# Two chained attentions and a three-expert maximum layer: the first layer of batches 2 to 7 as a Strassen scheme of 33 matmuls a tile

## The chip, the cores and the metric

The kernel runs on one core of a Trainium2 chip. The metric is the time of one execution on the device, in microseconds (us). The engines are TensorE (PE, with its weight loads PEld), VectorE (DVE), ScalarE (ACT), GpSimd (POOL) and SyncE (SP), which issues all DMAs here.

## The reference

For each of 8 batches and 8 heads (576 tokens, 64 features), 32 packed queries `p` attend over `k` and `v`; then the 576 queries `q` attend over the 32 packed results, which serve as keys and values. The heads are laid side by side (512 features a token) and go through a layer of three experts, of which the elementwise maximum is kept, and an output layer.

```python
def sm_attn(qq, kk, vv):
    s = scale * np.matmul(qq, kk.transpose(0, 1, 3, 2))
    s = s - np.max(s, axis=-1, keepdims=True)
    a = np.exp(s)
    a = a / (np.sum(a, axis=-1, keepdims=True) + 1e-09)
    return np.matmul(a, vv)
p_packed = sm_attn(p, k, v)
out = sm_attn(q, p_packed, p_packed)
...
h = np.maximum(np.maximum(x @ w1, x @ w2), x @ w3)
return (h @ w_out).astype(np.float32)
```

The four weight matrices are 512 x 768 (three) and 768 x 512.

## The kernel before

**Tiling.** Everything is float32 in and out. `b` is the batch, `j` one of 6 tiles of 128 hidden features, `hf` a half of the tokens (288 = `HS`), `r` the parity of the head (4 even heads and 4 odd ones; 4 heads x 32 packed rows fill 128 partitions). The attention weights over the packed rows stand in `et` (`[128, 576]`, one for each parity), and the second product with the packed values is never formed: `project(b, j)` multiplies the packed values into the experts' weights instead (`pw`, 128 rows x 3 experts x 128 features, for each parity), and `layer_in(b, j)` multiplies `et` by that. So a tile of the first layer is, for each expert and each token half, a sum over the two parities.

**Three matmuls a product.** Each operand is split into a rounded part and a remainder of the type fp32r (`hi`, `lo`; the remainder is the operand less its rounded part): `a2h`, `a2l` from `et`, `ph`, `pl` from `pw`. A product of two operands is three matmuls of 128 x 128 x 288: hi hi, lo hi, hi lo. A tile has 3 experts x 2 halves x 2 parities = 12 products, 36 matmuls (line 475), into six PSUM banks, one for each expert and half. `maximum(b, j, hf)` copies expert 0's bank to SBUF (`r`) and joins the other two with a maximum on DVE (line 489): 2 copies and 4 joins a tile.

**The rest of a batch.** `halves` and `operands` form the operands `ya`, `yb`, `yc` of the output layer out of pairs of tiles; `layer_out` is a Strassen scheme already, 126 matmuls (line 544); `finish` joins its products and stores. For the next batch `scores`, `weigh`, `invert`, `spread`, `values`, `packed`, `queries` and `attend` make its attention meanwhile.

**Buffers.** PSUM has 8 banks: `ps_moe` gives single ones (4) to the first layer's sums, the output layer's products and some projections, `ps_big` gives two pairs to the scores, the other projections and the attention. SBUF tiles under one tag share a number of slots; tag `y` has 21.

**Order.** Each step is a generator that issues a few instructions at a time. Two strings of words, `START` and `LOOP`, written out as tables, say which generator goes on next: `N01` is `layer_in(b, 1)`, `E010` `maximum(b, 1, 0)`, `P`, `H`, `O`, `F`, `A`, `B` are `project`, `halves`, `layer_out`, `finish`, `weigh_and_turn` and `attend`; a letter `v`, `g` or `a` behind a word puts its elementwise instruction on DVE, POOL or ACT. Each engine takes its instructions strictly in this order and waits on semaphores. `START` holds batches 0 and 1 and the preparation of batch 2; `LOOP` runs six times, for the first layer and the output layer of batches 2 to 7 with the attention of the batch after.

```python
with tc.manual_schedule():
    run(START, 0)
    for b in range(2, B):
        run(LOOP, b)
```

Of the kernel before, what the change touches and what calls it, by code (L numbers as in the profile page):

```python
# [53 lines left out]
C22 B011v B001 E010 A11 A11 A10 A10 E010 Z11 B001v C21 C20 C21 C22 N00 B001v B011 E000 A10 A11 q10 A10v E000
q11 A11 N00 B011g B011 B011 V101 C20 C30 C30 w31 B011 Z10 E010 N01 V101 C21 C21 K1 C30 N00 w52 C31 K1v C32 C32
Q1 N00 E011 E001 B10 C31 w41 P02 P02 B11 C52 P10 P10 B10 w40 B11 k20 C40 C41 C31 P02 N01 E011 C30 N01 C31 P03
B10 P03 E001 E001 C41 N02 N02 E020 N02 C52 N02 E011 k21 N02 H00 w42 B10 B11 P10 E021 P03 S2 C40 E020 C40 N03
N03 N03 v21 C41 C41 C42 E020 B11 C42 B10 E021 C52 E030 C42 A20 A20 A21 A21 w50 C50 w51 B11 B11 B10 X2 X2 C50
C50 C51 N02 C52 N03 C40 C42 P04 C51 C50 B10 E030 E030 P11 B11 N03 B11g N03 C51 B10g P04 C51 P04 E031 N04 N04
N04 P05 E031 B11 v20 B11 E040v E040 B10 H01 H01v N04 N04 N04 E021 w61 C61 E031 P05 E041 P05 N05 N05 N05 E040  # L60
w60 C60 B10g B10 B11 H00 N10 C61 E041 P11 Z20 E050 H00v X2 C60 C60 E041 C61 E050 P11 V201 Z21 V201 N11 N11 K2
w64 N10 C61 E110v E110 E050 H01 H01 w65 C65 C65 N11 q21 N11 N10 K2 E100v N10 H04v H04 q20 Q2 N11 w62 N10 E111
E110 C60 W0v N10 W0v W0v W0 w63 W0 H02v H02 E101 C65 P13 H04v B20 E100 B21 E101 C65 W0 E111 E100 P12 N11 C62
# [628 lines left out]
```

## Time and profile before

| | |
|---|---|
| median of 3 runs | 467.01 us (466.97 to 467.24) |
| span of the profiled execution, first to last instruction | 464.4 us |
| its own time | not given apart from the span; the runs lie 2.6 us above it |
| instructions | 11561, of them 4724 matmuls |
| PEld, share of the span | 87% |
| HBM read and written | 41.94 MB and 9.44 MB, 111 GB/s over the span |
| share of the chain that ended last | PE 88%, DMA 5%, SP's queue 3%, DVE 3%, ACT 1% |

How to read it: a group's row names the line, the engine, the operation, output and inputs by the program's names, the shapes and the count; then the summed time in us, the mean of one in ns, and the idle time before them with what ended it. Rows of the timeline begin with the start and the length in us. The chain is followed back from the last instruction to what released each. A row by stretch has the stretch, its length, then the busy time and count of PE, PEld, DVE, ACT and POOL, the granted clock, the DMA share and GB/s.

### The profile page before, as it was taken

The page shows a single profiled execution, that of the slowest core. Times are in us where ns is not written, and L with a number is a line of the kernel's source. Part 1 is how long each engine was busy: PE and PEld are TensorE (multiplying, and loading weights), DVE is VectorE, ACT ScalarE, POOL GpSimd, SP SyncE. Part 2 cuts the span into 40 slices and gives each one's busy share as a digit, 9 for nine tenths or more (in the row PEclk, how much of TensorE's full clock was granted, in tenths as well). Part 3 has the DMA queues.
Part 4 walks back from the last instruction along what each step waited for, and adds up shares of the span by engine and source line. Part 5 has one row for each costly group of instructions (what it writes and reads, how often), then busy time and mean ns, then how long its engine had stood idle before and what let it go on. Part 6 is the DMA issues. An engine that isn't in the chain of part 4 may idle for free.

```text
span 464.4 us, 11561 instructions
## 1 busy us (share of the span) xinstructions
PE 455.2 (98%) x4724; PEld 404.9 (87%) x4724; DVE 333.5 (72%) x698; ACT 159.9 (34%) x341; POOL 247.9 (53%) x213
## 2 busy tenths in 40 slices
PE   7999998999999999999999999999999999999996
PEld 3477887899899898998899988998989988998996
DVE  1799987888887678566887479766786668845552
ACT  2787856535322126022331025121260223302130
POOL 0468875574542675526572384706764275725832
PEclk9999999999999999999999999999999999999999
DMA  8999846010316430256004450065202540020002
GB/s 313 398 382 355 321 98 230 1 58 25 95 66 195 135 119 1 80 160 233 2 27 152 87 211 2 27 199 155 94 1 94 151 116 1 28 76 1 2 6 97
DMA packets 35780, 55.66 MB, mean 120 GB/s; under 512 B 17296, under 2 KB 26512, under 8 KB 35728
## 3 DMA queue, kind: packets, MB, share of 16 engines
q1 hardware_dynamic: 35728, 54.93, 35.4%
q8 instruction: 37, 0.61, 0.5%
q14 instruction: 15, 0.12, 0.1%
HBM read 41.94 MB, written 9.44 MB: 111 GB/s over the span
## 4 chain that ended last, share of the span: by engine, by line
PE 88%; DMA 5%; SPq 3%; DVE 3%; issue 1%; ACT 1%; DVEq 0%
PE mi L475 44%; PE mo L544 29%; PE pw L439 6%; PE idle L143 2%; SPq L319 2%; PE s L366 2%; PE av L337 2%; DMA wi<-in_wi 2%; PE s L253 2%; DMA q<-in_qt 1%; DMA kt<-in_kp 1%; PE tp L296 0%; DMA xt<-x 0%; SPq L159 0%; PE pa L337 0%
## 5 line engine op out<-in xcount | busy, mean ns | idle before, releaser
L475 PE MATMUL mi<-a2h,ph 128*128 128x288 f32 x576 | 173.5, 301 | 0.8 <-DVE pl L452 0.6
L475 PE MATMUL mi<-a2l,ph 128*128 128x288 f32 x576 | 169.9, 295 | 0.0
L475 PE MATMUL mi<-a2h,pl 128*128 128x288 f32 x576 | 169.6, 295 | 0.0
L489 DVE TENSOR_TENSOR r<-mi,r 128x288 f32<-128x288 f32 x192 | 84.4, 452 | 57.8 <-PE mi L475 55.3
L475 PEld LDWEIGHTS mi<-a2h,ph 128*128 128x128 f32 x576 | 108.0, 188 | 13.4 <-issue 7.0
L475 PEld LDWEIGHTS mi<-a2l,ph 128*128 128x128 f32 x576 | 108.0, 188 | 0.2
L475 PEld LDWEIGHTS mi<-a2h,pl 128*128 128x128 f32 x576 | 108.1, 188 | 0.0
L513 POOL TENSOR_TENSOR r<-r 128x288 f32<-128x288 f32 (+1 forms) x47 | 50.4, 1083 | 81.3 <-DVE r L489 65.5
L129 ACT COPY r<-mi 128x288 f32<-128x288 f32 x73 | 29.0, 399 | 185.8 <-PE mi L475 185.7
L450 ACT ACTIVATE ph<-pw 128x384 fp32r<-128x384 f32 (+1 forms) x67 | 40.2, 631 | 46.5 <-PE pw L439 43.5
L452 DVE SCALAR_TENSOR_TENSOR pl<-pw,ph 128x384 fp32r<-128x384 f32 (+1 forms) x67 | 46.2, 713 | 9.5 <-ACT ph L450 9.2
L544 PE MATMUL mo<-ych,xl 128*128 128x288 f32 x144 | 42.5, 295 | 0.0
L544 PE MATMUL mo<-ych,xh 128*128 128x288 f32 x144 | 42.4, 294 | 0.0
L544 PE MATMUL mo<-ycl,xh 128*128 128x288 f32 x144 | 42.3, 294 | 0.0
L439 PE MATMUL pw<-w_sb,pt 64*32 64x384 f32 x768 | 36.3, 487 | 0.1
L206 POOL TENSOR_TENSOR w_sb<-w_sb,wi 128x512 int32<-128x512 int32 x18 | 23.9, 1336 | 22.0 <-DVE w_sb L202 17.4
L134 POOL TENSOR_TENSOR ybl<-r,ybh 128x576 fp32r<-128x576 f32 x15 | 21.7, 1448 | 19.7 <-DVE ybh L131 16.2
L134 POOL TENSOR_TENSOR ycl<-r,ych 128x864 fp32r<-128x864 f32 x12 | 26.6, 2218 | 5.1 <-PE mi L475 2.4
L544 PE MATMUL mo<-yah,xh 128*128 128x288 f32 x96 | 28.9, 301 | 0.0
L544 PE MATMUL mo<-yal,xh 128*128 128x288 f32 x96 | 28.4, 296 | 0.2 <-DVE yal L134 0.2
L544 PE MATMUL mo<-ybh,xh 128*128 128x288 f32 x96 | 28.3, 295 | 0.0
L544 PE MATMUL mo<-yah,xl 128*128 128x288 f32 x96 | 28.3, 295 | 0.0
(123 smaller groups left out, 808.4 us busy)
## 6 DMA issues: line engine op xcount, KB each, us to landing
kt<-in_kp SPq DMA_DIRECT2D x16, 640.0 KB, 5.4
q<-in_qt SPq DMA_DIRECT2D x16, 576.0 KB, 5.6
wi<-in_wi SPq DMA_DIRECT2D x18, 512.0 KB, 8.6
v<-in_va SPq DMA_DIRECT2D x16, 512.0 KB, 5.7
wi<-in_wo SPq DMA_DIRECT2D x6, 512.0 KB, 6.7
out_t<-r SPq DMA_DIRECT2D x8, 288.0 KB, 2.2
out_t<-t SPq DMA_DIRECT2D x8, 288.0 KB, 2.3
out_t<-s SPq DMA_DIRECT2D x8, 288.0 KB, 2.7
```

Of the source, the lines that this page charges most:

```text
L129: e.copy(out=out, in_=src)
L134: on(default).tensor_tensor(out=lo, in0=src, in1=hi.bitcast(F32), op=ALU.subtract)
L143: nc.tensor.matmul(out=ps[:, 0:n * P], lhsT=ident, rhs=ident.unsqueeze(1).to_broadcast([P, n, P]), start=True, stop=True,)
L206: nc.gpsimd.tensor_tensor(out=dst.bitcast(I32), in0=dst.bitcast(I32), in1=up, op=ALU.add)
L253: nc.tensor.matmul(out=s1[b][r][32 * n:32 * n + 32, hf, 0:HS], lhsT=kt[g][o, w:w + NP], rhs=kt[g][o, pr * S + hf * HS:pr * S + (hf + 1) * HS],
L439: nc.tensor.matmul(out=ps[r][NP * n:NP * n + NP, 0:NW * P], lhsT=pt_sb[b % 2][o, NP * n:NP * n + NP], rhs=w_sb[o, j, n * NW * P:(n + 1) * ...
L450: nc.scalar.activation(out=hi[:, r], in_=x, func=AF.Copy, scale=2.0 ** -WS)
L452: nc.vector.scalar_tensor_tensor(out=lo[:, r], in0=x, scalar=2.0 ** -WS, in1=hi[:, r].bitcast(F32), op0=ALU.mult, op1=ALU.subtract,)
L475: nc.tensor.matmul(out=sums[b, j, hf, x][:, 0:HS], lhsT=w[:, r, x * P:(x + 1) * P], rhs=a[:, c], start=(r == 0 and n == 0), stop=(r == R - ...
L489: nc.vector.tensor_tensor(out=h, in0=sums[b, j, hf, i][:, 0:HS], in1=h, op=ALU.max)
L513: less = lambda out, x, y: on("g").tensor_tensor(out=out, in0=x, in1=y, op=ALU.subtract)
L544: nc.tensor.matmul(out=ps[:, 0:HS], lhsT=w[:, x, m * P:(m + 1) * P], rhs=h[:, z], start=(p == 0 and i == 0), stop=(p == NQ - 1 and i == 2),)
```

## The change

For batches 2 to 7 (`b >= FAST`), experts 0 and 1, the two parities and the two token halves are taken as a 2 x 2 block product and computed with 7 products in place of 8 (Strassen's scheme in Winograd's form); expert 2 keeps its 4. A tile is then 11 products, 33 matmuls. What goes with it:

- `replace(j)`, once for each tile: in `w_sb`, expert 1's weights of the even heads become expert 0's less expert 1's (64 x 512).
- `project` also makes float32 copies `pf` of experts 0 and 1 on ACT, three combinations of 128 x 128 for each tile, and their split `sh`, `sl`.
- `differences(b)`: four instructions overwrite the halves of `et` by differences, which are split as `th`, `tl`.
- `layer_in_fast` fills five banks a tile: `e` (expert 2, half 0), `x`, `u`, `y`, `f` (expert 2, half 1). Some are read while they are filled: after its first two products `e` is copied to `h[0]`, then ACT writes x's first product into it, and PE adds expert 0's second product to that.
- `maximum_fast` does it in 4 copies and 6 joins a tile. A term that two sums share is added after their maximum.
- `START` and `LOOP` are written anew, with other engines for many elementwise steps.

```diff
+    def replace(j):
+        w = w_sb[0:64, j].rearrange("p (n i x) -> p n i x", n=4, i=NW)
+        on("g").tensor_tensor(out=w[:, :, 1], in0=w[:, :, 0], in1=w[:, :, 1], op=ALU.subtract)
+        yield 0
...
     def project(b, j):
...
+        if b >= FAST:
+            f = pool.tile([P, R, 2 * P], F32, name=f"pf{b}_{j}", tag="y", bufs=NY)
+            for r, x in zip(parts, src):
+                nc.scalar.activation(out=f[:, r], in_=x[:, :, 0:2 * P], func=AF.Copy, scale=2.0 ** -WS)
+                yield 1
...
+        combine(1, 3, 1, ALU.subtract)
+        yield 1
+        combine(0, 0, 1, ALU.add)
+        yield 1
+        combine(2, 2, 1, ALU.subtract)
+        yield 1
+        hi = pool.tile([P, 3, P], F32R, name=f"sh{b}_{j}", tag="y", bufs=NY)
+        copy(hi, f[:, 0:3])
+        yield 1
+        lo = pool.tile([P, 3, P], F32R, name=f"sl{b}_{j}", tag="y", bufs=NY)
+        split_lo(lo, f[:, 0:3], hi)
...
+    def differences(b):
+        e = [loaded["et", b, r] for r in range(R)]
+        c = slice(0, HS), slice(HS, S)
+        def less(r, h, x, y):
+            on("g").tensor_tensor(out=e[r][:, c[h]], in0=e[x[0]][:, c[x[1]]], in1=e[y[0]][:, c[y[1]]], op=ALU.subtract)
+        less(0, 0, (0, 1), (0, 0))
+        less(0, 1, (1, 1), (0, 1))
+        less(1, 1, (1, 1), (0, 0))
+        less(1, 0, (1, 0), (1, 1))
+        for r in range(R):
+            hi = pool.tile([P, S], F32R, name=f"th{b}_{r}", tag="y", bufs=NY)
+            copy(hi, e[r])
+            lo = pool.tile([P, S], F32R, name=f"tl{b}_{r}", tag="y", bufs=NY)
+            split_lo(lo, e[r], hi)
...
+    def layer_in_fast(b, j):
+        def product(ps, w, x, first=False):
+            for n, (wi, xi) in enumerate(((0, 0), (1, 0), (0, 1))):
+                nc.tensor.matmul(
+                    out=ps[:, 0:HS], lhsT=w[wi], rhs=x[xi], start=first and n == 0, stop=n == 2,
...
+        product(e, a(0, 2), v(0, 0), first=True)
+        product(e, a(1, 2), v(1, 0))
+        product(x, a(0, 0), v(0, 0), first=True)
+        product(u, a(0, 1), t(0, 1), first=True)
+        product(bank("y"), s(2), v(1, 1), first=True)
+        product(x, s(1), t(1, 1))
+        product(e, a(1, 0), v(1, 0))
+        product(u, a(1, 1), t(1, 0))
+        product(x, s(0), t(0, 0))
+        product(f, a(0, 2), v(0, 1), first=True)
+        product(f, a(1, 2), v(1, 1))
...
+    def maximum_fast(b, j):
+        copy(h[0], of("e"))
+        copy(of("e"), of("x"))
+        copy(h[1], of("u"))
+        join(h[1], of("y"), h[1])
+        copy(u, of("x"))
+        join(h[0], of("e"), h[0])
+        join(u, of("u"), u, ALU.add)
+        join(h[0], u, h[0])
+        join(h[1], of("x"), h[1], ALU.add)
+        join(h[1], of("f"), h[1])
...
-S1 A10 N00 E000 A11 N01 v10 E010v A10 N00 N00 N00 N00 N00 X1 A11 X1 v11 N02 N02 N02 N02 N02 E000 X1 Z10 E001
+S1 A10 A10 N00 N00 E00a A11 N00 N00 q11 P05 E00a A11 N00 N00 E00v E00 E00a N00 N00 N01 N00 X1 X1 E00 E00 E00g
```

(Between the calls of the new functions stand yields, one a word of the table.)

The order on PE, in the pass of batch 4, tile 4, after the matmuls `s2` of the next batch's queries. Before, six matmuls in a row fill one bank (`mi`, with batch, tile, half, expert):

```order
L366 MATMUL s2_5_1_3957<-q11_3868,pt1_74 32x288 x4
L475 MATMUL mi4_4_1_0_3967<-a2h4_0_3511,ph4_4_3850 128x288
L475 MATMUL mi4_4_1_0_3967<-a2h4_0_3511,pl4_4_3851 128x288
L475 MATMUL mi4_4_1_0_3967<-a2l4_0_3551,ph4_4_3850 128x288
L475 MATMUL mi4_4_1_0_3967<-a2h4_1_3444,ph4_4_3850 128x288
L475 MATMUL mi4_4_1_0_3967<-a2h4_1_3444,pl4_4_3851 128x288
L475 MATMUL mi4_4_1_0_3967<-a2l4_1_3495,ph4_4_3850 128x288
```

After, three at a time go to the banks `mx`, `mu`, `my`, and then to `mx` a second time:

```order
L373 MATMUL s2_5_1_4163<-q11_3801,pt1_74 32x288 x4
L530 MATMUL mx4_4_4172<-a2h4_0_3622,ph4_4_4071 128x288
L530 MATMUL mx4_4_4172<-a2h4_0_3622,pl4_4_4072 128x288
L530 MATMUL mx4_4_4172<-a2l4_0_3665,ph4_4_4071 128x288
L530 MATMUL mu4_4_4188<-th4_0_3708,ph4_4_4071 128x288
L530 MATMUL mu4_4_4188<-th4_0_3708,pl4_4_4072 128x288
L530 MATMUL mu4_4_4188<-tl4_0_3716,ph4_4_4071 128x288
L530 MATMUL my4_4_4197<-a2h4_1_3643,sh4_4_4176 128x288
L530 MATMUL my4_4_4197<-a2h4_1_3643,sl4_4_4194 128x288
L530 MATMUL my4_4_4197<-a2l4_1_3669,sh4_4_4176 128x288
L530 MATMUL mx4_4_4172<-th4_1_3721,sh4_4_4176 128x288
```

The second visit to `mx` now stands behind six matmuls of other banks, and waits for ACT's copy of `mx` into `me`.

The order on DVE, at the same place of the pass. Before:

```order
L452 SCALAR_TENSOR_TENSOR pl4_5_3890<-pw4_5_3763,ph4_5_3889 128x768
L489 TENSOR_TENSOR r4_1_3714<-mi4_3_1_2_3914,r4_1_3714 128x288
L489 TENSOR_TENSOR r4_2_3887<-mi4_4_0_1_3923,r4_2_3887 128x288
L489 TENSOR_TENSOR r4_2_3887<-mi4_4_0_2_3930,r4_2_3887 128x288
L389 STREAM_TRANSPOSE e5_1_4002<-s2_5_0_3948 128x288
L389 STREAM_TRANSPOSE e5_1_4002<-s2_5_1_3957 128x288
L389 STREAM_TRANSPOSE e5_0_4020<-s2_5_0_3948 128x288
L389 STREAM_TRANSPOSE e5_0_4020<-s2_5_1_3957 128x288
L393 TENSOR_REDUCE m2_5_0_0_4023<-e5_0_4020 128x18
L395 TENSOR_TENSOR e5_0_4020<-e5_0_4020,m2_5_0_0_4023 128x576
```

After:

```order
L396 STREAM_TRANSPOSE e5_1_4183<-s2_5_0_4154 128x288
L396 STREAM_TRANSPOSE e5_1_4183<-s2_5_1_4163 128x288
L400 TENSOR_REDUCE m2_5_1_0_4186<-e5_1_4183 128x18
L574 TENSOR_TENSOR r4_2_4180<-my4_4_4197,r4_2_4180 128x288
L574 TENSOR_TENSOR r4_2_4180<-me4_4_4133,r4_2_4180 128x288
L574 TENSOR_TENSOR u4_4_4209<-mu4_4_4188,u4_4_4209 128x288
L396 STREAM_TRANSPOSE e5_0_4231<-s2_5_0_4154 128x288
L396 STREAM_TRANSPOSE e5_0_4231<-s2_5_1_4163 128x288
L574 TENSOR_TENSOR r4_2_4180<-u4_4_4209,r4_2_4180 128x288
L574 TENSOR_TENSOR r4_2_4180<-mx4_4_4172,r4_2_4180 128x288
L574 TENSOR_TENSOR r4_2_4180<-mf4_4_4224,r4_2_4180 128x288
```

The joins of a tile are six, one of them (`r<-u,r`) between two SBUF tiles, and the attention's transposes are parted among them.

The order on POOL from one batch's output layer into the next batch's first layer. Before:

```order
L590 TENSOR_TENSOR u_3_3471<-u_3_3471,t_3_3437 128x576
L592 TENSOR_TENSOR t_3_3437<-v_3_3508,t_3_3437 128x576
L513 TENSOR_TENSOR r4_0_3584<-r4_0_3584 128x288
L131 CAST yah4_0_3745<-r4_0_3584 128x576
L134 TENSOR_TENSOR yal4_0_3754<-r4_0_3584,yah4_0_3745 128x576
```

After:

```order
L736 TENSOR_TENSOR u_3_3624<-u_3_3624,t_3_3564 128x576
L738 TENSOR_TENSOR t_3_3564<-v_3_3705,t_3_3564 128x576
L141 TENSOR_TENSOR tl4_0_3716<-et4_0_3620,th4_0_3708 128x576
L141 TENSOR_TENSOR tl4_1_3723<-et4_1_3638,th4_1_3721 128x576
L473 TENSOR_TENSOR pf4_1_3544<-pf4_1_3544 128x128 x3
L138 CAST sh4_1_3729<-pf4_1_3544 128x384
L473 TENSOR_TENSOR pf4_2_3535<-pf4_2_3535 128x128 x2
L141 TENSOR_TENSOR sl4_1_3733<-pf4_1_3544,sh4_1_3729 128x384
L138 CAST sh4_2_3735<-pf4_2_3535 128x384
L141 TENSOR_TENSOR sl4_2_3737<-pf4_2_3535,sh4_2_3735 128x384
```

Eleven instructions for the new operands stand between the output layer's last sums and the first difference of `r4_0`.

More of the change, by code (lines that the diff above doesn't have):

```diff
@@ L36 @@
 WS = 8
+FAST = 2
 NX, NB, NY = 6, 8, 21
@@ L54 @@
[L54 to L63, printed above, removed]
@@ L85 @@
+P10 P10 P10 B10 H04g O0 O0 P05 P05 B10v B11a H05a H05v H05g H05v P12 P12 H03a F0 P11 P10g H05a B10 F0 P10g
+H03v O0 F0 O0 F0 P10g B11 B10v O0 O0 H05v O0 F0 F0 P10a P10g B10 B10a F0 O0 F0 B11g B11 P11 B11a O0 O0 B10g
+T1v T1v B11v T1v T1g k20 O0 O0 O0 F0 F0 T1a P12 P12g P11 F0 F0 T1g F0 F0 T1a T1g F0 P11g P11g P11g P11g P12g
+P12g P11g P12g P11 P11 P12g P12 P12 P12 P11 O0 F0
 """
@@ L455, in project, with combine @@
             yield 1
-    sums, hidden, hid = {}, {}, {}
+        if b < FAST:
+            return
+        f = f.rearrange("p r (i x) -> p (r i) x", i=2)
+        def combine(k, x, y, op):
+            on("g").tensor_tensor(out=f[:, k], in0=f[:, x], in1=f[:, y], op=op)
+        combine(1, 3, 1, ALU.subtract)
[5 more added lines that the diff above has]
+        hi = pool.tile([P, 3, P], F32R, name=f"sh{b}_{j}", tag="y", bufs=NY)
@@ new lines, in maximum_fast, with join @@
+    def maximum_fast(b, j):
+        if (b, j // 2) not in hidden:
+            hidden[b, j // 2] = pool.tile([P, 4, HS], F32, name=f"r{b}_{j // 2}", tag="b", bufs=NB)
+        h = [hidden[b, j // 2][:, 2 * (j % 2) + hf] for hf in range(2)]
+        of = lambda name: sums[b, j, name][:, 0:HS]
+        def join(out, x, y, op=ALU.max):
+            nc.vector.tensor_tensor(out=out, in0=x, in1=y, op=op)
+        copy(h[0], of("e"))
+        yield 0
+        copy(of("e"), of("x"))
+        yield 0
+        copy(h[1], of("u"))
+        yield 0
+        join(h[1], of("y"), h[1])
+        yield 0
+        u = pool.tile([P, HS], F32, name=f"u{b}_{j}", tag="y", bufs=NY)
+        copy(u, of("x"))
+        yield 0
+        join(h[0], of("e"), h[0])
+        yield 0
+        join(u, of("u"), u, ALU.add)
+        yield 0
+        join(h[0], u, h[0])
+        yield 0
+        join(h[1], of("x"), h[1], ALU.add)
+        yield 0
+        join(h[1], of("f"), h[1])
+        yield 0
@@ L459, in layer_in @@
     def layer_in(b, j):
+        if b >= FAST:
+            yield from layer_in_fast(b, j)
+            return
         p_hi, p_lo = pw[b, j]
@@ L479, in layer_in, with maximum @@
                 yield 0
-    def maximum(b, j, hf):
+    def maximum(b, j, hf=None):
+        if b >= FAST:
+            yield from maximum_fast(b, j)
+            return
         if (b, j // 2) not in hidden:
@@ L613, in fused_kernel @@
         "B": attend, "C": convert, "P": project, "N": layer_in, "E": maximum, "H": halves,
-        "O": layer_out, "F": finish, "W": weights,
+        "T": differences, "R": replace, "O": layer_out, "F": finish, "W": weights,
     }
@@ L631, in run @@
                 continue
-            if kind not in "wCW":
+            if kind not in "wCWR":
                 x[0] += base
```

88 lines of the change are left out of this document (66 added, 22 removed).

## The prediction

> **What bounds the kernel now.** I read the page first, for the balance of the engines, then the chain that ended last.
>
> ```profile
> PE 455.2 (98%) x4724; PEld 404.9 (87%) x4724; DVE 333.5 (72%) x698; ACT 159.9 (34%) x341; POOL 247.9 (53%) x213
> ```
>
> The page alone does not prove that PE is the bound, since its matmuls are pipelined. The chain in order of time does. One pass of the loop over batches, from one batch's scores to the next, reads:
>
> ```profile
> 303.82 1.13 PE s L253 x32
> 304.95 14.51 PE mi L475 x108
> 319.46 2.10 PE pw L439 x48
> 321.56 1.39 PE av L337 x80
> 322.95 2.56 PE mi L475 x18
> 325.51 0.11 PE av L352
> 325.62 4.76 PE mi L475 x36
> 330.39 1.13 PE s L366 x32
> 331.52 7.36 PE mi L475 x54
> 338.88 2.10 PE pw L439 x48
> 340.97 16.87 PE mo L544 x126
> 357.85 1.13 PE s L253 x32
> ```
>
> Every piece is PE and each begins where the last ended: a pass is 54.03 us of matmuls without a hole. The pace is 14.51/108 = 0.134 us a matmul, not the 0.295 us that the groups show as the length of one: that is latency. Next, the busy time by stretch, for a pass and for the end of the opening:
>
> ```profile
> 303.82:357.85 54.03, 54.03 (x592) 49.31 (x598) 38.45 (x81) 14.63 (x34) 28.51 (x24) 1.00 0.33 102
> 100.00:120.00 20.00, 20.00 (x153) 20.00 (x152) 16.02 (x32) 7.49 (x14) 10.41 (x10) 1.00 0.14 49
> 120.00:140.00 20.00, 20.00 (x184) 18.53 (x183) 18.22 (x32) 6.78 (x13) 11.06 (x8) 1.00 0.28 93
> ```
>
> After the length come PE, PE's weight loads, DVE, ACT and POOL. In a pass DVE has 15.6 us left over, POOL 25.5, ACT 39.4. The granted clock is 1.00. What the change takes comes off the bound; what it adds must fit into those remainders.
>
> Prices of single instructions, by form, and two joins back to back:
>
> ```profile
> L489 DVE TENSOR_TENSOR r<-mi,r 128x288 f32<-128x288 f32 x192 | 84.4, 452 | 57.8 <-PE mi L475 55.3
> L129 ACT COPY r<-mi 128x288 f32<-128x288 f32 x73 | 29.0, 399 | 185.8 <-PE mi L475 185.7
> L450 ACT ACTIVATE ph<-pw 128x384 fp32r<-128x384 f32 x38 | 16.7, 495 | 41.0 <-PE pw L439 41.0
> L452 DVE SCALAR_TENSOR_TENSOR pl<-pw,ph 128x384 fp32r<-128x384 f32 x38 | 19.0, 538 | 9.2 <-ACT ph L450 9.2
> L513 DVE TENSOR_TENSOR r<-r 128x288 f32<-128x288 f32 x14 | 7.0, 501 | 0.0
> L134 DVE TENSOR_TENSOR yal<-r,yah 128x576 fp32r<-128x576 f32 x10 | 8.2, 818 | 0.5 <-ACT yah L129 0.5
> L134 DVE TENSOR_TENSOR ycl<-r,ych 128x864 fp32r<-128x864 f32 x12 | 12.6, 1054 | 0.0
> L134 POOL TENSOR_TENSOR yal<-r,yah 128x576 fp32r<-128x576 f32 x14 | 20.3, 1449 | 2.5 <-ACT yah L129 1.6
> L218 POOL TENSOR_TENSOR xt<-xb,xt 128x256 f32<-128x256 f32 x2 | 1.5, 739 | 0.8 <-DVE xl L134 0.8
> L129 ACT CAST yah<-r 128x576 fp32r<-128x576 f32 x11 | 7.4, 674 | 2.8 <-PE mi L475 2.1 <-DVE u L563 0.7
> L266 DVE TENSOR_REDUCE mx<-s 128x1 f32<-128x576 f32 x16 | 12.0, 752 | 11.6 <-PE s L253 11.6
> L271 ACT ACTIVATE a<-s,nm 128x576 f32<-128x576 f32 x16 | 11.8, 744 | 7.2 <-DVE nm L267 7.2
> L313 DVE STREAM_TRANSPOSE x<-a 128x576 f32<-128x576 f32 x12 | 8.9, 771 | 0.0
> 221.31 0.81 DVE L489 TENSOR_TENSOR r<-mi,r 128x288 f32<-128x288 f32 x2
> ```
>
> The pair takes 0.81 us and one 0.45, so in a row a 288-column DVE instruction costs a step of 0.37; I take 0.08 off the others likewise.
>
> **The change, part by part.** *Products.* 36 becomes 33 matmuls a tile, six tiles a batch, six batches: 18 x 0.134 = 2.4 us a pass, 14.5 us in all, on the path directly. An all-hidden remainder would give 467.0 - 14.5 = 452.5.
>
> *DVE, a pass.* Joins go from 24 to 36: 12 x 0.37 = 4.5. Two more copies from PSUM: 0.7. Three half-differences of the attention weights at 0.42: 1.3. Four 128-column combinations at 0.2 (an estimate, the step scaled by columns; ends 0.1 and 0.4): 0.8. One split of a combination 0.5, one more `r<-r` 0.4, one each more of `yal`, `ybl`, `ycl`: 0.7 + 0.7 + 1.0. Two casts leave for ACT: -0.9. Sum 9.7, so 38.45 + 9.7 = 48.1 of a pass of 51.6: 93%.
>
> *POOL, a pass.* 14 combinations at 0.45 (estimate between 0.37, half the 256-column row, and 0.74): 6.3. Five splits at 1.05 (between the 0.74 and 1.45 rows): 5.2. Two `tl` at 1.45, two casts and a difference: 4.9. Five casts, four splits and an `r<-r` leave: -9.8. So 28.5 + 6.6 = 35.1, 68%.
>
> *ACT, a pass.* Ten more PSUM copies at 0.4, nine `pf` at 0.45 (between the 0.40 and 0.50 rows), thirteen casts new or taken over at 0.67: 4.0 + 4.1 + 8.7 = 16.8, so 31 of 51.6. Not a bound.
>
> *The new chain inside a tile.* Before, a product bank was filled once and read once. Now `e` is copied out, gets x's partial sum written into it by ACT, and is added to by PE; `u` and `x` are read between additions. PE is in order, so everything behind such a matmul waits. PE gives room of its own: between x's first product and its second stand `u` and `y`, 6 x 0.134 = 0.8 us, against two ACT copies of 0.4, of which the first starts 0.4 us sooner while x is computed. I laid the four orders of one pass side by side and added the rows' durations down them by hand, with 0.2 us from a last matmul's issue to its reader (0.16 of it is 0.295 less 0.134).
>
> Tile 0 as the example, in us from the end of the scores. PE: `e` to 0.8, `x` 1.2, `u` 1.6, `y` 2.0, projection P5 (2.10/3) 2.7, second `x` 3.1, third part of `e` 3.5, second `u` 3.9, third `x` 4.3, tile 1's `e` 5.1, `f` 5.9, tile 1's `x` 6.3. ACT: exponential 1.0 to 1.8, copy of `e` to 2.1, `e<-x` to 2.5; PE's second `x` comes at 2.7: room 0.2. DVE: two maxima with a small instruction each to 1.9, copy of `u` 2.2, join of `y` 2.6, two transposes 4.0, joins of `e` 4.4, `u` 4.8, `r<-u,r` 5.3, `x` 5.7, which frees a bank that PE wants at 6.3: room 0.6. Behind that `x` stand on DVE the copy of tile 1's `e`, which ACT waits for before it can fill that bank, and the join of `f`.
>
> Room at most such places is 0.1 to 0.6 us. It is negative at four: the two banks behind the projection P3, where ACT issues two `pf` and two `ph` (about 1.5 us) and DVE two `pl` (0.54 each) before PE gets them back: 0.1; the second bank of P4, which waits for DVE's `r<-mx` of tile 2: 0.35; the banks behind P4: 0.3; the first output product, which waits for tile 5's joins behind an `e<-e,m`: 0.15. Sum 0.9 us a pass. Ends: 0 and all 2.4.
>
> *DVE held by POOL.* This trace shows something that speaks against the change:
>
> ```profile
> 62.15 2.85 POOL L134 TENSOR_TENSOR a2l<-et,a2h 128x576 fp32r<-128x576 f32 x2
> 64.16 1.45 DVE L134 TENSOR_TENSOR yal<-r,yah 128x576 fp32r<-128x576 f32 x1
> 103.93 0.75 DVE L395 TENSOR_TENSOR e<-e,m 128x576 f32<-128x576 f32 x1
> 223.94 2.31 POOL L513 TENSOR_TENSOR r<-r 128x288 f32<-128x288 f32 x2
> 225.60 1.26 DVE L395 TENSOR_TENSOR e<-e,m 128x576 f32<-128x576 f32 x1
> 445.59 1.37 DVE L134 TENSOR_TENSOR ybl<-r,ybh 128x576 fp32r<-128x576 f32 x1
> ```
>
> The split at 64.16 ended at 65.61, 0.61 after POOL's ended at 65.00; the subtraction at 225.60 took 1.26 beside POOL and 0.75 at 103.93 without. Of the 26 DVE instructions with two SBUF operands that started while POOL ran, 14 (the first at 64.16, the last at 445.59) were held, all with 0.24 us or more of a POOL tensor-tensor still to go. A pass has 8 such DVE instructions and loses 0.5 us to this; it will have 26, and POOL goes from 28.5 to 35.1: 0.5 x 26/8 x 35.1/28.5 = 2.0 us. With it DVE is at 50.1 of 51.6. A hold-up costs PE only where the room is smaller than it; of the 2.0 I take 0.2, ends 0 and 2.0. The Trainium skill (SBUF — State Buffer, section "SBUF: two separate sides") has the pair of ports that DVE and POOL share as an exclusive lock for the whole instruction; by that rule the trace agrees, each of the 14 waits lasted to POOL's end.
>
> *The opening.* The first two batches keep their 36 products. It gets DVE net 4.9: four differences of attention weights 1.7, four `pf` combinations 0.8, four weight differences at 0.6 (estimate between the 288 and 576-column rows) 2.4; splits and casts that move between DVE, POOL and ACT come out even. The two stretches above have 5.8 us of DVE left, but most additions stand in the second, which has 1.8: some 3 us run over into the first pass, whose DVE has 3.5 left. Ends 0 and 4.9; I take 1.0. Today's loop begins here:
>
> ```profile
> 141.74 1.13 PE s L253 x32
> ```
>
>
> *The last pass* has no attention work beside it, and the way out of its first layer is the old one:
>
> ```profile
> 443.58 0.46 DVE r L489
> 444.04 0.68 DVE yal L134
> 444.76 15.89 PE mo L544 x118
> ```
>
> PE waits 1.2 us there, for a join and a split. The split goes from DVE to POOL, 0.7 longer, but it needs tile 4 alone, and 8 matmuls of the output layer (1.07 us) stand ahead of the one that reads it; I leave the wait as it is and take 0.2 for what remains of the other waits: 2.4 - 0.2 = 2.2 saved. SP's queue gets no DMA; the `xt` transfers follow the same two transposes, one join later in DVE's order.
>
> *Sum.* Five passes of 2.4 - 0.9 - 0.2 = 1.3: 6.6 with the unrounded 2.42. Last pass 2.2, opening -1.0: 7.8 us. The profiled span is 464.4, so 456.6; the median of the runs, 467.01, lies 2.6 above the span, which I carry over: 459.2.
>
> **Rivals.** *Everything hides.* For it: 0.1 to 0.6 us of room at most places, and a wait that shifts PE once also gives the next ones room. Against: 93% of DVE. Below 455, down to 452.5; chance 0.13.
>
> *The bank releases eat the gain.* 36 releases a pass at 0.067 us are 2.4 us. For it: the four negative places; an error of 0.1 us in what I take for a reader's delay would make half the others negative. Against: a late matmul gives the readers time. 465 to 469; chance 0.13.
>
> *DVE becomes the bound through POOL's hold.* If the 26 fall at random on POOL's 68%, each loses half a POOL instruction (35.1/39 = 0.9): 26 x 0.68 x 0.45 = 8.0 us, DVE 56.1, a pass 2.1 longer than today; five of them, 10.4 - 2.2 + 1.0: 476. It decides from 54.0 - 48.1 = 5.9 us of hold a pass. Against: today's 8 lose 0.5 and at random would lose 8 x 0.53 x 0.6 = 2.5. Chance 0.12. By the Trainium skill's rule (same section) nothing softens this: the one that starts first keeps the ports.
>
> **How the numbers follow.** My own case, 455 to 465, gets 0.62. A difference under 0.2% (0.9 us) is about what cannot be told from no change. Faster by more: my case, full hiding, and a little of the bank case: 0.80. Same: 0.06, from the bank case. Slower: POOL's hold and the bank case's end: 0.14. The range leaves out the bottom of full hiding (0.05) and most of the slower cases (0.13): 453.5 to 468.
>
> **What would show it.** A pass of about 52.7 us between two batches' scores; 4616 matmuls; DVE at 47 to 50 us a pass, POOL near 35; PE idle of about 1 us a pass put down to DVE `r<-mx`, `pl` and `r<-my`. Wrong: pieces of DVE longer than 1 us in the chain of a pass, `r<-u,r` well over 0.5 us on average (POOL's hold), or a loop that begins later than 142.7.

## The result and the profile after

The changed kernel takes 471.78 us (median of 4 runs, 470.56 to 473.20) against 466.99 us for the kernel before, run beside it (4 runs, 466.92 to 467.24): 1.0105 times as long, 95% interval 1.0082 to 1.0129. The prediction was 459.2 us, with a range from 453.5 to 468.0. The profiled execution took 473.20 us with a span of 471.4, 7.0 more than before; it is the slowest of the four, and the spans of the others are 468.8 to 470.0.

The engines over the whole span:

```profile
PE 457.4 (97%) x4616; PEld 393.2 (83%) x4616; DVE 392.1 (83%) x856; ACT 250.3 (53%) x536; POOL 279.8 (59%) x292
```

The 108 matmuls that the scheme saves are gone, 4616 in place of 4724. Next come the stretches from one batch's scores to the next, five passes and then the last with the end (stretch, length, then PE, PEld, DVE, ACT, POOL):

```profile
143.32:196.85 53.53, 53.53 (x573) 47.25 (x580) 47.38 (x105) 29.29 (x66) 33.45 (x37) 1.00 0.35 103
196.85:251.04 54.19, 54.03 (x573) 47.28 (x579) 48.06 (x105) 29.08 (x65) 34.43 (x40) 1.00 0.35 102
251.04:306.65 55.61, 54.49 (x574) 47.52 (x581) 48.30 (x105) 29.08 (x65) 34.34 (x40) 1.00 0.36 99
306.65:362.42 55.77, 54.54 (x573) 47.54 (x579) 47.52 (x105) 29.12 (x65) 34.42 (x40) 1.00 0.34 99
362.42:417.00 54.58, 54.07 (x567) 47.45 (x567) 48.27 (x105) 29.02 (x65) 34.34 (x40) 1.00 0.26 77
417.00:471.40 54.40, 47.77 (x373) 43.74 (x371) 33.31 (x71) 19.55 (x45) 28.09 (x31) 1.00 0.11 39
```

A pass was 54.03; now the five are 53.5 to 55.8, and the last pass with the end is 54.4 in place of 52.5. The busy times are what was forecast: DVE 47.4 to 48.3, POOL 33.5 to 34.4, ACT 29. PE's busy time counts its short stalls as busy (53.53 of 53.53), so I cut each pass by the starts of the matmuls: the time from the first of a block to the first of the next, summed by kind, in us.

| | before | pass 1 | 2 | 3 | 4 | 5 |
|---|---|---|---|---|---|---|
| products of the first layer (216, now 198) | 29.29 | 28.03 | 28.44 | 28.42 | 28.50 | 28.50 |
| projections `pw` (96, in 2 groups, now 4) | 4.19 | 4.92 | 4.91 | 4.90 | 4.89 | 4.91 |
| `av` | 1.41 | 1.41 | 1.70 | 3.17 | 3.25 | 2.14 |
| scores, both | 2.26 | 2.26 | 2.26 | 2.26 | 2.26 | 2.26 |
| output layer | 16.87 | 16.90 | 16.89 | 16.85 | 16.88 | 16.75 |

With 18 x 0.134 = 2.41 us less the products would take 26.88. They take 1.2 to 1.6 more, the projections 0.7 more, and `av` up to 1.8 more. The chain that ended last shows that third one, in pass 3 (start, length, what):

```profile
253.17 0.41 PE mx L530 x3
253.58 0.17 SPq L181
...
253.79 0.75 SPq L172
...
255.15 8.63 DMA v<-in_va
263.78 0.02 issue
263.80 0.59 SPq L326
...
270.00 1.92 DMA xt<-x
271.92 0.14 issue
272.06 1.41 PE av L344 x74
```

PE's `av` waits for the last of 16 `xt` transfers. SP issues them one after another at some 0.65 us, and ahead of the seventh it stood still for 2.3 us, until a v load of 8.6 us had landed. SP's waits at these issues, before and after (wait in us, times, longest), and the landing of v (count, KB, median us):

```profile
SPq L319 <- DMA v<-in_va: 0.5, 1, 0.5
v<-in_va SPq DMA_DIRECT2D x16, 512.0 KB, 5.7
```

```profile
SPq L326 <- DMA v<-in_va: 10.1, 9, 2.3
v<-in_va SPq DMA_DIRECT2D x16, 512.0 KB, 7.9
```

### The profile page after: what moved, and what is told of

It is laid out like the page before. It is cut to its first block, busy times and chain, and to the rows that moved or that the text cites. A ratio compares the mean times of both kernels' runs of the same rounds, so it can differ in the third digit from the quotient of the medians.

```text
span 471.4 us, 11957 instructions
## 1 busy us (share of the span) xinstructions
PE 457.4 (97%) x4616; PEld 393.2 (83%) x4616; DVE 392.1 (83%) x856; ACT 250.3 (53%) x536; POOL 279.8 (59%) x292
## 4 chain that ended last, share of the span: by engine, by line
PE 76%; DMA 10%; SPq 5%; DVE 3%; ACT 2%; issue 2%; POOL 1%; POOLq 0%; DVEq 0%; ACTq 0%
PE mo L690 27%; PE mi L617 9%; PE mx L530 7%; PE me L530 6%; PE pw L446 6%; DMA v<-in_va 5%; PE mf L530 4%; PE mu L530 4%; SPq L326 4%; PE my L530 3%; PE idle L150 2%; PE s L373 2%; PE s L260 2%; PE av L344 2%; DMA wi<-in_wi 2%
## 5 line engine op out<-in xcount | busy, mean ns | idle before, releaser
L141 POOL TENSOR_TENSOR sl<-pf,sh 128x384 fp32r<-128x384 f32 x30 | 32.5, 1093 | 42.0 <-ACT sh L136 24.6
L473 POOL TENSOR_TENSOR pf<-pf 128x128 f32<-128x128 f32 x80 | 37.5, 481 | 13.8 <-ACT pf L456 12.5
L617 PE MATMUL mi<-a2h,ph 128*128 128x288 f32 x144 | 44.3, 307 | 1.2 <-DVE r L635 1.2
L617 PE MATMUL mi<-a2h,pl 128*128 128x288 f32 x144 | 42.5, 295 | 0.3 <-DVE pl L464 0.3
L617 PE MATMUL mi<-a2l,ph 128*128 128x288 f32 x144 | 42.5, 295 | 0.0
L617 PEld LDWEIGHTS mi<-a2h,ph 128*128 128x128 f32 x144 | 27.0, 188 | 8.6 <-issue 2.3
L530 PE MATMUL me<-a2h,ph 128*128 128x288 f32 x108 | 32.7, 303 | 0.0
L530 PE MATMUL me<-a2h,pl 128*128 128x288 f32 x108 | 31.9, 295 | 0.0
L530 PE MATMUL me<-a2l,ph 128*128 128x288 f32 x108 | 31.8, 294 | 0.0
L690 PE MATMUL mo<-ybl,xh 128*128 128x288 f32 x96 | 28.3, 295 | 0.0
```

The lines of the kernel that those rows point to most:

```text
L141: on(default).tensor_tensor(out=lo, in0=src, in1=hi.bitcast(F32), op=ALU.subtract)
L473: on("g").tensor_tensor(out=f[:, k], in0=f[:, x], in1=f[:, y], op=op)
L530: nc.tensor.matmul(out=ps[:, 0:HS], lhsT=w[wi], rhs=x[xi], start=first and n == 0, stop=n == 2, skip_group_check=not first,)
L617: nc.tensor.matmul(out=sums[b, j, hf, x][:, 0:HS], lhsT=w[:, r, x * P:(x + 1) * P], rhs=a[:, c], start=(r == 0 and n == 0), stop=(r == R - ...
L690: nc.tensor.matmul(out=ps[:, 0:HS], lhsT=w[:, x, m * P:(m + 1) * P], rhs=h[:, z], start=(p == 0 and i == 0), stop=(p == NQ - 1 and i == 2),)
```

## The experiments

Each kernel ran beside the kernel before on the same chip; the median of that one was 466.5 to 467.1 us each time, and the ratios are taken against it. Kernels are compared by the cut of their passes as well, since the time at which the loop begins varies from profile to profile (see e5). How far one profile's passes can be trusted is seen where two kernels have the same program in passes 1 to 5 and differ in the last alone (e6 and e9, e7 and e8, e12 to e15): passes 1 and 5 agree within 0.1 us, passes 2 to 4 differ by up to 0.9. The passes, in us, and the last pass from its first product to its first output product:

| kernel | time | ratio to before, interval | loop begins | passes 1 to 5 | last |
|---|---|---|---|---|---|
| before | 467.0 | | 141.7 | 54.0 54.0 54.0 54.0 53.9 | 31.7 |
| after | 471.8 | 1.0105 (1.0082 to 1.0129) | 143.3 | 53.5 54.2 55.6 55.8 54.6 | 32.7 |
| e1 | 469.0 | 1.0050 (1.0032 to 1.0068) | 143.5 | 53.5 54.0 54.0 54.4 53.9 | 32.6 |
| e2 | 472.3 | 1.0120 (1.0094 to 1.0146) | 142.7 | 54.1 54.6 54.7 55.7 54.5 | 33.0 |
| e3 | 474.1 | 1.0162 (1.0132 to 1.0192) | 142.7 | 54.7 54.8 54.8 56.2 54.7 | 32.6 |
| e5 | 469.3 | 1.0055 (1.0032 to 1.0077) | 144.2 | 54.1 54.1 54.1 54.1 54.0 | 31.7 |
| e6 | 466.6 | 0.9985 (0.9970 to 0.9999) | 142.4 | 53.2 54.1 53.1 54.0 53.0 | 32.8 |
| e7 | 472.1 | 1.0107 (1.0091 to 1.0122) | 143.6 | 53.9 54.2 53.9 55.1 53.8 | 33.8 |
| e8 | 471.1 | 1.0105 (1.0082 to 1.0127) | 143.9 | 53.9 53.9 53.9 54.6 53.8 | 33.8 |
| e9 | 471.3 | 1.0094 (1.0079 to 1.0109) | 142.6 | 53.2 53.5 53.1 53.2 53.1 | 38.8 |
| e10 | 470.1 | 1.0079 (1.0057 to 1.0102) | 143.5 | 53.1 53.2 53.1 53.3 53.1 | 37.0 |
| e11 | 468.6 | 1.0048 (1.0033 to 1.0062) | 141.3 | 54.4 54.6 54.4 54.4 54.3 | 32.0 |
| e12 | 467.4 | 1.0000 (0.9979 to 1.0021) | 142.9 | 53.2 53.3 53.2 53.7 53.0 | 34.8 |
| e13 | 465.3 | 0.9975 (0.9957 to 0.9992) | 141.8 | 53.1 53.2 53.5 53.8 53.1 | 32.7 |
| e14 | 467.2 | 1.0012 (0.9993 to 1.0031) | 142.2 | 53.1 53.3 53.4 53.2 53.1 | 34.2 |
| e15 | 467.1 | 1.0008 (0.9993 to 1.0022) | 144.6 | 53.1 53.2 53.2 53.6 53.1 | 34.1 |

**e1: the q load behind the `xt` transfers.** The new table has the word `q11` ahead of `v11` and `v10`; the old one had it behind the `xt` issues.

```diff
-        nc.sync.dma_start(out=loaded["q", b, g][:, :, c], in_=...)
+        later.append((out, in_))        # for g == 1 of batches 3 to 7
...
         (end of spread, behind the 16 xt transfers)
+        for out, in_ in later: nc.sync.dma_start(out=out, in_=in_)
```

> The changed kernel with one load moved on SyncE's queue: the q load of 576 KB that the new loop issues ahead of the v loads now stands behind the 16 xt transfers. Theory A (the xt transfers are late because a q load and four v loads share the bandwidth just ahead of them, the v loads then take 8 us, and the fifth to ninth xt issue wait for them): av stops waiting in passes 2 to 6 of the loop, which gives back the 0.2, 1.75, 1.85 and 0.75 us that the 80 av products took over 1.39 us, and the wait ahead of them; about -4.5 us, 467.3 us, with SyncE's wait for v at the xt issues (10.1 us) under 3 us. Theory B (the q load was hidden, xt is late because DVE writes x late): 471.8 us, the first xt issue is still 5.5 us into a pass and av at 19.3. Theory C: the q load is now late for the scores that read it at 25 us of the pass, 470 to 474 us.

469.04 us, 2.7 faster than the changed kernel. SP's wait, v's landing and the same place of pass 3 in the chain:

```profile
SPq L332 <- DMA v<-in_va: 1.7, 2, 1.2
v<-in_va SPq DMA_DIRECT2D x16, 512.0 KB, 6.1
```

```profile
257.23 1.61 DVE r L583 x2
...
269.20 1.18 PE pw L455 x16
270.38 1.39 PE av L353 x80
```

`av` takes 1.39 in every pass and the five passes are 3.9 us shorter in sum; the scores that read q do not wait. Theory A holds in that this load made `xt` late; whether the v loads were slow because they shared bandwidth with it or because they stood behind it in the queue is not separated. (The time gained less because this profile's loop began 0.25 later and because the changed kernel's profile was of its slowest run.) But the passes are then 53.5 to 54.4 with 18 fewer matmuls each: the gain of the products is still eaten elsewhere.

**e2: one trip to the projections fewer, on top of e1.**

```diff
-... N00 N00 q11 P05 E00a A11 ... E01v P03 P03 P03 N01 ...
+... N00 N00 q11 E00a A11 ... E01v P05 P03 P03 P03 N01 ...
```

> The kernel of e1, and the weight projections of tile 5 (16 short matmuls) stand beside those of tile 3 instead of in a group of their own 3.3 us into the pass. Theory A (each trip of TensorE from the long products to the short projections and back costs about 0.35 us: the last product 0.14, the first projections 0.1, the first product after 0.1, which my sum left out): one group fewer in 6 passes, 2 us faster than e1, about 465.3 us if e1 gives 467.3. Theory B (the trips lie in time in which TensorE waits anyway): the same as e1 within 0.3 us.

472.34 us, 3.3 slower than e1, where both theories had it faster or the same. PE's rows at that place, first in the changed kernel, then in e2:

```profile
254.29 0.88 PE L446 MATMUL pw<-w_sb,pt 64*32 64x384 f32 x16
255.10 0.40 PE L530 MATMUL mx<-th,sh 128*128 128x288 f32 x1
```

```profile
254.47 0.29 PE L539 MATMUL my<-a2l,sh 128*128 128x288 f32 x1
255.34 0.40 PE L539 MATMUL mx<-th,sh 128*128 128x288 f32 x1 [0.58 <-ACT me L136]
```

The projections of tile 5 filled a hole: the second `x` product waits for ACT's copy out of its bank in any case. Without this filler PE waits 0.6 us there. So the trip is paid in time in which PE would wait, and this run cannot price the trip itself.

**e11: the price of the trip, in the kernel before,** where nothing waits on the other engines.

```diff
-... A10 N00 N00 N00 N00 N00 X1 ... H00g N01 H00 N02 P05 E011v ...
+... A10 N00 N00 P05 N00 N00 N00 X1 ... H00g N01 H00 N02 E011v ...
```

> The kernel before (36 products), and the 16 short projections of tile 5 stand alone, about 4 us into a pass, in place of beside those of tiles 3 and 4. Theory A (a trip from the long products to the short projections and back costs TensorE about 0.35 us, which my sum for the changed kernel, with two such trips more in a pass, left out): 0.3 to 0.4 us a pass, about 2.1 us slower than before, 469.2 us, since nothing waits on the other engines here. Theory B (such a trip costs nothing): 467.1 us.

468.61 us, 2.1 slower than before, as theory A has it. Each pass is 0.40 longer; its chain is matmuls without a hole:

```profile
251.52 3.36 PE mi L475 x24
254.88 0.81 PE pw L439 x16
255.69 11.34 PE mi L475 x84
267.03 1.49 PE pw L439 x32
268.51 1.39 PE av L337 x80
```

24 + 84 products take 14.70 here and took 14.51 before, the 48 projections 2.30 and took 2.10: 0.2 on either side of the switch. The changed kernel makes two such trips more in a pass, 0.8 us by this price.

**e3 and e6: VectorE held by GpSimd.** On top of e1 the sum `u` stays in its PSUM bank, in all tiles (e3) or in tiles 0 to 4 (e6).

```diff
-        join(u, of("u"), u, ALU.add)
+        t = u if j == NJ - 1 else of("u")      # e3: t = of("u") in all tiles
+        join(t, of("u"), u, ALU.add)
         yield 0
-        join(h[0], u, h[0])
+        join(h[0], t, h[0])
```

> The kernel of e1, and the sum u = mu + u is written into its PSUM bank instead of SBUF, so that the maximum that reads it has one SBUF operand in place of two. Theory A (DVE instructions with two SBUF operands are held while GpSimd works; r<-u,r has a mean of 582 ns here against 455 for the others, 4.7 us over 36): the mean falls to about 455 ns, and the 0.4 us that TensorE waits at mu in four passes goes; 1 to 2 us faster than e1. Theory B (the bank of mu is kept one DVE instruction, 0.45 us, longer, 36 times, and TensorE waits for it): 2 to 8 us slower than e1. Theory C: both small, the same as e1 within 0.3 us.

> The kernel of e1 with the edit of e3 in tiles 0 to 4 only; in tile 5 the sum stays in SBUF, so that the bank that the next batch's first projections wait for is free one DVE instruction earlier. Theory A (in e3 the hold by GpSimd was gone and gave 0.86 us a pass by 34 us into it, and all that e3 lost, 1.57 us a pass, is the wait of the 48 projections for the last bank of tile 5): the 0.86 us of each pass stays won and the 48 projections take 2.1 us again: 469.0 - 5 x 0.86 = 464.7 us. Theory B (the later release costs in the other tiles too, where e3 hid it behind the wait at the end): 469 us or more.

The instruction that reads `u`, by groups in the changed kernel and in e6 (30 with one PSUM operand, 6 as before):

```profile
L574 DVE TENSOR_TENSOR r<-u,r 128x288 f32<-128x288 f32 x36 | 21.0, 582 | 0.5
```

```profile
L583 DVE TENSOR_TENSOR r<-mu,r 128x288 f32<-128x288 f32 x30 | 13.4, 448 | 0.5
L583 DVE TENSOR_TENSOR r<-u,r 128x288 f32<-128x288 f32 x6 | 2.7, 446 | 0.0
```

and one that was held, in pass 3 of the changed kernel, beside what ran on GpSimd:

```profile
257.10 1.02 POOL L141 TENSOR_TENSOR sl<-pf,sh 128x384 fp32r<-128x384 f32 x1
```

```profile
257.19 1.24 DVE L574 TENSOR_TENSOR r<-u,r 128x288 f32<-128x288 f32 x1
```

It started 0.09 after GpSimd's split and ended 0.31 after it. With a PSUM operand the mean is 448 ns beside the same GpSimd work; that agrees with the Trainium skill (SBUF — State Buffer, section "SBUF: two separate sides"), which names two SBUF inputs as a condition of the lock. In e6 a pass falls from 53.99 to 53.14 (pass 3 of each): 0.42 and 0.08 less from the start of a `mu` and a `mx`, some 8 us into the pass, to the block behind each, 0.25 at the third group of projections, 0.11 at a later `mu`. The first product behind that `mu`, in e1 and in e6:

```profile
259.71 0.37 PE L539 MATMUL my<-a2h,sh 128*128 128x288 f32 x1 [0.16 <-DVE r L583]
```

```profile
257.91 0.37 PE L539 MATMUL my<-a2h,sh 128*128 128x288 f32 x1
```

e6 is at 466.58 us, 2.5 under e1, and 464.7 was expected. Passes 3 and 5 got the 0.86 us and pass 1 got 0.26; the last pass got nothing. Pass 2 lost its gain at `av`, by late `xt` (see e13). Pass 4 lost it elsewhere, five us into the pass, where PE waits 0.5 us for a copy that stands behind an exponential on ScalarE, and this one waits for an output store of the batch before:

```profile
307.78 0.74 ACT L284 ACTIVATE a<-s,nm 128x576 f32<-128x576 f32 x1 [1.01 <-DMA out_t<-t]
```

e3 shows the other half. It has the same gains by 34 us into the pass, and then the projections of the next batch wait for the last bank of tile 5 (1.57 us a pass):

```profile
286.37 0.83 PE L455 MATMUL pw<-w_sb,pt 64*32 64x384 f32 x2
287.94 0.56 PE L455 MATMUL pw<-w_sb,pt 64*32 64x384 f32 x8 [0.74 <-DVE r L583]
```

One VectorE instruction of 0.45 us more on a bank costs more than three times that here. Theory A of e6 holds in its mechanism, and in the size in passes 3 and 5.

**e13 (and e10): the first v load earlier, on top of e6.** The word `v11` moves into the pass before, ahead of its last output stores.

> The kernel of e6 with the first v load issued in the pass before, ahead of the last output stores, and nothing else. Theory A (the 1.0 us that av waits in passes 2 and 4 of e6 is the xt issue that waits for a v load): all passes 53.1 to 53.3 us as in e10, about 1.5 us faster than e6, 465 us. Theory B: the same as e6, 466.6 us.

Its time is 465.31 us, ratio 0.9975 (0.9957 to 0.9992): the fastest of all, and faster than before; by its interval not told apart from e6. Passes 2 and 4 fall from 54.1 and 54.0 to 53.2 and 53.8, pass 3 rises by 0.3; what is left of pass 4 are products that wait, its `av` takes 1.41. The theory is borne out in pass 2 alone: there `av` takes 1.4 us in all five kernels with the moved load (e10, e12 to e15), and 1.6 to 2.6 in the four of this line without it (e6 to e9). In pass 4 `av` takes 1.5 us in e6 and was not what waited, and e9, which has e6's program up to the last pass, is at 53.2 there with the load where it was. e10 is the same with the edit of e9:

> The kernel of e9, and the first of a pass's two v loads is issued in the pass before, ahead of its last output stores. Theory A (what is left of av's wait in e6, 1.0 us in passes 2 and 4, is xt issues that wait for the v load eight transfers earlier): av takes 1.39 us in every pass, 1 to 2 us faster than e9. Theory B (the wait is left, because the second v load or DVE's x sets it): within 0.3 us of e9.

All its passes are 53.1 to 53.3, but those of e9 were 53.1 to 53.5 already: of the 1.2 us that it is faster than e9, 0.2 lie in the five passes and the rest in the last one, so that its time does not decide between the theories. Its 470.07 us come from the edit of e9 in the last pass, which takes 37.0.

**e5: the opening's order without its added work.** The old loop behind the new table `START`, without the words `R` and `T`.

> The kernel before with the order of work of the new opening (first two batches), but without the work that the opening prepares for the new scheme (weight differences and score differences); the loop is the old one. Theory A (the loop begins 1.6 us later in the changed kernel because of the added work): 467.0 us, loop begins at 141.7 us. Theory B (because of the new order of the opening): 468.5 us, loop begins at 143.3 us.

469.30 us, 2.7 above the kernel before though the passes are the old ones within 0.1 us, and the loop begins at 144.2: taking the work out does not bring the 1.6 us back, so theory A falls. How much of them is the order is not settled by one profile: in the thirteen kernels with the new opening (in some a load or a projection's steps differ at its end) the loop begins between 141.8 and 144.6, in the middle at 142.9; with the old one at 141.7 and, in e11, 141.3. e13 and e15 have the same opening, and 141.8 and 144.6.

**e7: `ph` ahead of `pf`, on top of e6.**

```diff
-        for each half: pf;  then for each half: ph, pl
+        for each half: ph;  then for each half: pf, pl
```

> The kernel of e6, and ScalarE writes ph ahead of pf after each projection of the new scheme, so that VectorE's pl, the last reader that frees the projection's bank, starts up to 0.66 us earlier. Theory A (in each pass the third group of projections and the products behind it wait for pl: DVE waited 6.4 us in all for ph): 0.2 to 0.4 us a pass and about 0.6 us in the last pass, where no av stands ahead of the products: 1.5 to 2.5 us faster than e6. Theory B (the banks are then held by pf instead, and the combinations made from pf come later for the y products): the same as e6 or up to 1 us slower.

472.09 us, 5.5 slower than e6: against theory A, and far beyond theory B's "up to 1 us". Passes are 0.1 to 1.0 longer, 3.3 in sum; in pass 3 the block ahead of a later tile's `mf` takes 0.40 more and that `mf`, ahead of the scores, 0.22 more. The last pass is 1.0 longer, and the loop begins 1.2 later, which can be chance (see e5). The wait at `mf`, which is for a join:

```profile
276.03 0.41 PE L543 MATMUL mf<-a2h,ph 128*128 128x288 f32 x1 [0.24 <-DVE r L587]
```

Why the joins come later is not shown. e8 adds one engine choice to it:

> The kernel of e7, and in the last pass alone the low part of ya of the third pair is made by VectorE (0.75 us) and not GpSimd (1.42 us); the output products wait for it there, since no projections of a next batch stand between. Theory A (that step ends the wait of 1.2 us at the second output product): 0.5 to 0.7 us faster than e7. Theory B (VectorE is still joining tile 5 then, and its own queue delays it): the same within 0.3 us.

Its median is 471.14 us, 0.95 under e7, but the intervals of the two lie over each other. From the first to the last output product it takes 17.50 us in place of 17.74: 0.24, less than the 0.5 expected. The cast that the split reads, and the split:

```profile
447.69 0.67 ACT L136 CAST yah<-r 128x576 fp32r<-128x576 f32 x1 [1.32 <-DVE r L673]
```

```profile
448.87 0.75 DVE L141 TENSOR_TENSOR yal<-r,yah 128x576 fp32r<-128x576 f32 x1
```

The split starts 0.51 us after the cast's end, behind two joins of tile 5, as theory B has it in part.

**The last pass: e9, e12, e14, e15.** In the changed kernel, a product near the start of that pass, PE's third group of projections there and the two products behind it that wait, and then the chain at the output layer:

```profile
419.13 0.40 PE L530 MATMUL mu<-tl,ph 128*128 128x288 f32 x1 [0.59 <-POOL tl L141]
...
434.14 0.88 PE L446 MATMUL pw<-w_sb,pt 64*32 64x384 f32 x16
435.57 0.40 PE L530 MATMUL mx<-a2h,ph 128*128 128x288 f32 x1 [0.56 <-DVE r L574]
...
436.79 0.40 PE L530 MATMUL mu<-th,ph 128*128 128x288 f32 x1 [0.55 <-DVE pl L464]
```

```profile
449.59 0.69 ACT yah L136
...
450.35 1.42 POOL yal L141
...
451.81 1.19 PE mo L690 x7
```

The first row is a wait for GpSimd's split `tl`: that `mu` takes 1.25 us, and 0.40 at its place in pass 1, where the scores of the next batch stand ahead of it. No run was made on it.

e9 and e12 give the projections of tiles 3 and 4 other banks in that pass; e12 keeps the steps of the table, e9 does not, so that the other engines' work moves with it there and its last pass says little.

```diff
+            if j and b == B - 1:      # e12
+                x = ps_big.tile([P, R, 512], F32, ...); ps = [x[:, r] for r in range(R)]
+            else:
                 ps = [ps_moe.tile(...) for r in range(R)]
```

> The kernel of e6, and in the last pass alone the projections of tiles 3 and 4 go to the pair of PSUM banks that scores and av use in the other passes, not to two of the four banks through which the products rotate. Theory A (the last pass is longer than before because the products wait for pl, which frees the projections' banks, and no av and no scores stand between to cover it: the third group takes 1.2 us in place of 0.8, mx behind it 1.45 in place of 0.5, mx and mu after that 0.85 and 0.65 in place of 0.4 each): 1.5 to 2 us faster than e6. Theory B (the joins themselves are late in the last pass, whatever the projections hold): within 0.3 us of e6.

> The kernel of e6 with the first v load issued in the pass before (as in e10), and with the projections of tiles 3 and 4 of the last pass in the pair of banks that scores and av use elsewhere, now written in the same steps as before (in e9 fewer steps moved the engines' other work of that pass too). Theory A (the last pass is slow because pl frees the banks of these projections late): the 32.75 us from the last pass's first product to its first output product fall to about 31, and the time is 1.5 to 2 us under that of the kernel without that edit, about 463.5 us. Theory B (the joins are late themselves): the same as without it within 0.3 us.

In e12 the group takes 0.81 (1.22 in e13) and `mx` behind it 0.49 (1.44): the bank waits go, as theory A says. But `y` behind them then takes 2.50 in place of 0.47, and the pass is 2.1 longer than e13's. The wait, in e12:

```profile
431.15 0.40 PE L543 MATMUL mx<-th,sh 128*128 128x288 f32 x1 [1.94 <-ACT me L136]
```

The two halves share one PSUM tile now, `ph` of the second waits for `pl` of the first, and ACT's copy that `mx` needs stands behind it. So this edit takes one wait away and makes another; it does not show what the pass would take without either. e14 moves `ph`, `pl` and the combinations of tile 5 behind the joins of tile 3:

> The kernel of e13, and in the last pass alone ScalarE's ph and VectorE's pl of tile 5 (about 0.9 and 1.0 us), with tile 5's weight combinations, stand some 12 VectorE instructions later, behind the first joins of tile 3 rather than ahead of them. Theory A (in the last pass the products of tiles 3 and 4 wait for banks that VectorE frees late, because the steps of tiles 4 and 5 queue ahead of its joins and no av covers them): the 0.95 us that mx waits behind the third group of projections, and the 0.43 and 0.25 us of mx and mu four us later, shrink by about 1 us in all; 464.3 us. Theory B (what TensorE waits for there is tile 3's own joins and pl of tile 4, not the queue): the same as e13 within 0.3 us, 465.3 us.

> The kernel of e14, and in the last pass the low part of ya of the third pair on VectorE in place of GpSimd, as in e8. Theory A (VectorE has room for it before the last low part of yb): 0.3 to 0.6 us faster than e14. Theory B: the same within 0.3 us.

e14 is at 467.17 us, 1.9 slower than e13, which neither theory has. In e14:

```profile
426.65 0.40 PE L539 MATMUL mx<-a2h,ph 128*128 128x288 f32 x1 [0.34 <-DVE r L583]
...
428.09 0.40 PE L539 MATMUL mu<-th,ph 128*128 128x288 f32 x1 [0.78 <-DVE pl L473]
...
432.58 0.40 PE L539 MATMUL mf<-a2h,ph 128*128 128x288 f32 x1 [0.99 <-DVE r L583]
```

The 1.44 from `mx` to `mu` stay, against theory A, and a `mf` four us later comes 1.15 later, for a join that now has the moved steps ahead of it. e15 differs from e14 by 0.05 us in time; from the first to the last output product it is 0.2 shorter, as in e8. So it is not the queue of tile 5's steps. Joins of the tile before, and `pl` of tile 4, are what PE waits for; that they are uncovered because `av` (1.4 us) does not stand there, as it does in the other passes, is argued from the rows and was not shown by a run.

## Why the prediction was wrong

The forecast span was 456.6, the profiled one 471.4: 14.8 us. By its own steps:

- *Products.* 18 matmuls fewer a pass: right, 4616 in all. *DVE, POOL, ACT*: 50.1 with the hold (48.1 without), 35.1 and 31 forecast; 47.4 to 48.3 with the hold in it, 33.5 to 34.4 and 29 measured. These sums were 1 to 3 us too high, and DVE did not become the bound.
- *The projections: the step that left out a term.* In the example of tile 0 projection P5 is put down as 2.10/3, a third of a group. It is a trip of its own, at 0.40 (e11). Two more a pass, in five passes: 4.0 us by that price. I read the order of PE and not that a block's price in the chain holds for one long block. e2 adds that the trip is not simply waste: PE would wait at that place.
- *"SP's queue gets no DMA; the xt transfers follow the same two transposes, one join later in DVE's order": the step that failed.* It counted DMAs and not their order. A q load of 576 KB had come ahead of the v loads; v landed in 7.9 us and not 5.7, and the `xt` issues waited for v. `av` takes 4.6 us more over five passes; e1 gives 3.9 us of pass time back with that one load.
- *Bank releases, 0.9 a pass, and POOL's hold, 0.2 a pass.* Products and projections lose 1.9 to 2.3 us a pass; less 0.8 for the trips it is 1.1 to 1.5, against 1.1. The sum is close, but the split was not. With the hold of `r<-u,r` taken off (e6, passes 1, 3 and 5) products and projections lose 1.5 to 1.6, less the trips 0.7 to 0.8, so that the 0.9 for bank releases was about right. The hold of DVE itself was put too high: of 130 such instructions in five passes, the 30 `r<-u,r` took 4.0 us more than 0.45 each, and five `r<-r` of 288 columns 0.87 in place of 0.45, together 6.1 us, 1.2 a pass, where 2.0 stood. Its cost to PE was put too low: 0.3 to 0.9 us a pass went with one instruction (e6, the same passes), against 0.2. Two thirds of the hold lay on `r<-u,r`, and the frees of two banks stand behind that; the sign for "wrong" that I named, its mean well over 0.5 us, is what came (582 ns).
- *The opening.* 1.0 forecast, 1.6 in the profile, 1.3 in the middle of thirteen: within its ends, but by luck as far as the runs show. The term stood for VectorE's added work, and e5, without that work, is no earlier.
- *The last pass.* 2.2 us saved was forecast; it is 1.8 longer (471.4 - 416.9 against 464.4 - 411.7). I did not lay that pass out by itself. I subtracted 0.2 for waits, and 3.2 us came with the products, the price of two trips among them; 0.85 of it is the wait for `tl` near its start. The covers of the other passes, scores and `av`, are missing there, which is argued from the rows. I took the end as it was, and the stretch from the first output product on is 0.8 longer. There I had read the 1.2 us of the chain's join and split as PE's wait; PE issued 8 output matmuls meanwhile, and the step over the wait was 0.44 us. It is 1.22 now. The 8 matmuls (1.07 us) did not cover the split, since it did not stand ready: the difference and the cast that it needs come behind joins of tile 5 in VectorE's order, so that it began 0.70 us after the first output product (450.35 and 449.65) and took 1.42. Back on VectorE it gives 0.24 (e8, e15).

Added: 4.0 + 4.6 + about 1.5 of further waits in five passes, 4.0 in the last, 0.6 in the opening are 14.7. The transfers, the trip and the hold are shown by runs (e1, e11, e6); the last pass and the opening stay open. Of the rivals none came alone: bank releases and the hold took what they were given between them, and the two largest terms of the five passes, the trips and the transfers, stood in no rival.
